# An order of single operations written out as a table, in place of a planner's, in a one-core attention and gated-MLP kernel

## The chip, the cores and the metric

One Trainium2 core. TensorE (PE) multiplies matrices, VectorE (DVE) and ScalarE (ACT) work on elements, GpSimd (POOL) does element work on SBUF alone, SyncE (SP) issues all the transfers. The metric is the device time of one execution in microseconds (us); lower is better.

## The reference

```python
# B = H = 4, S = 1088, D = 32, r = 8, d_model = 128, d_ff = 1024
a, b = S1 @ x, S2 @ x                       # 8 features each, per position
phi(x) = outer(a, b).reshape(64)
kv  = einsum('bhsf,bhsd->bhfd', phi(k), v);  z = phi(k).sum(s)
num = einsum('bhsf,bhfd->bhsd', phi(q), kv); den = phi(q) . z + 1e-6
x   = (num / den) -> (B, S, 128)
h   = relu(x @ w_in);  u, v = h[..., :512], h[..., 512:]
v_n = (v - mean(v)) / sqrt(var(v) + 1e-6)
v_s = einsum('ts,bsd->btd', w_spatial, v_n) + b_spatial
out = (u * v_s) @ w_out
```

## The kernel before

**Arithmetic.** Every product of the MLP is made in three matmuls: each factor is a rounded high part and the remainder as a low part (names in h and l: `wih`/`wil`, `xh`/`xl`, `vh`/`vl`, `wTh`/`wTl`), and high x high, high x low and low x high are summed in PSUM. `mm3` is that for products of x (L516 to L518); for the mixing of positions with `w_spatial` the three are L1092, L1094 and L1101. `w_in`, `w_out` and the S matrices arrive as 64-bit floats and are turned into 32-bit ones on the chip: for each half of `w_in` one ACT operation (the absolute value, L577) and six on VectorE (L580 to L590), then the split (L594 the high part, L526 the low).

**Stages.** For batch 0 (`attention0`): keys are projected (L674), copied by ACT (L679) and multiplied out to features on VectorE (L681, 128x768 a piece); a matrix product with v gives the 64 x 33 sums; queries the same way, turned by PE (L800), the quotient on VectorE (L818 to L833). Then the hidden v half for batch 0: `pv` products (L516 to L518 with `wi`), ReLU on ACT (L948), statistics on VectorE (L950), normalization and split into `vh` and `vl` (L1039 is vl's subtraction). With these, the mixing begins: `spatial` sums nine blocks of positions for each of 4 x 3 tiles (d, c) in a PSUM bank, `hidden` makes u (a bank `pu`, ACT's L1084 reads it), `gate` multiplies (L1128), `out_mm` multiplies with `w_out` (banks `po`). The attention of batch b+1 runs beside the mixing of batch b: `kv` (L724) sums keys with values on PE; a copy on ACT (L766), the four block products `kd` on VectorE (L907), a split into `kvh` (L594) and `kvl` (L526) follow, and then `nd` on PE (numerators and denominators, L516 with `area`) needs both. Query features are made on GpSimd: a product `fa` (L867) and the low part `fl` (L529). Batch 3 uses an algorithm with fewer products (`main_fast`).

**Order.** The code records operations, each with its engine, what it reads and writes. `schedule` then lists them in one order, and each engine runs its share of it in that order; PE fills some waits in the startup with small matmuls that nothing reads (L543), after N_WARM = 8 at the very start (L539). Before, `schedule` is a planner: it gives each operation a cost and a due time, `LEADS` moves due times by a few hundred numbers, and the operation that can start first goes next, the more urgent of two near each other. An operation marked `sh` reads two SBUF tiles on VectorE (or works in a mode of that sort); `pin` on a GpSimd operation adds a wait for the last `sh` operation ordered ahead of it, and is set for the query products of batches 2 and 3:

```python
s = max(s, shared_to + (66 if o.pin else -40))          # a GpSimd operation's planned start
...
o.behind = shared if o.pin else None                    # becomes a real wait
...
op("POOL", c_pool(n), ..., r=[fb], w=[fa], pin=b >= PIN_FROM)      # PIN_FROM = 2
```

SBUF and PSUM tiles live in groups of buffers (`po` 3, `sp` 2, `pu` 1, `sd` 2 in PSUM), used in turn.

Of the kernel before, what the change touches and what calls it, by code (L numbers as in the profile page):

```python
# [50 lines left out]
N_WARM = 8  # L51
# [23 lines left out]
SLACK = {'PE': 32, 'ACT': 56, 'DVE': 106, 'POOL': 890, 'SP': 84}  # L75

C_MM = {260: 120.5, 276: 127.0, 332: 146.8, 424: 186.8, "x1": 153.0, "rp": 150.5, 384: 174.7, 320: 146.0, 512: 231.5}
SETTLE = {332: (0, 5.1, 10.2, 14.5, 17.5, 20.1, 22.9, 24.8, 26.7, 28.3, 29.3, 30.3, 31.2, 31.7, 32.2), 424: (0, 6.4, 13.4, 18.1, 19.9, 21.9, 23.3, 24.3, 25.2, 25.6)}  # L80
STICK, PAUSE = 0.0, 30.0
HBM_LAG = (0, 500)
PIN_FROM, LATER = 2, 300.0

FILL_COLD, COLD_TO = 500, 7000
FILL, FILL_TO, FILL_SPARE = 430, 50.0, 150
FIRST_RATE, LOW_DELAY = 0.18, 4.4


class T:  # L90


    def __init__(self, k, tag, name, shape, dt):
        self.k, self.tag, self.name, self.shape, self.dt = k, tag, name, shape, dt
        self.users, self.left, self.free_at, self.slot, self._ap = [], 0, 0.0, None, None
        if tag is not None:
            k.fifo.setdefault(tag, []).append(self)

    @property
# [36 lines left out]
class Order:  # L136
# [13 lines left out]
    def op(self, eng, cost, fn, r=(), w=(), due=None, kb=0, alts=(), sh=False, kind=None, after=0.0, lead=0.0, f4=False, cls=None, lag=0.0, pin=False):  # L150
        o = Op()
        o.n, o.eng, o.fn, o.due, o.kb, o.f4 = len(self.ops), eng, fn, due, kb, f4
        o.lag, o.pin, o.behind = lag, pin, None
        o.cls, o.nmm = cls or ("f4" if f4 else "", 1)
        o.alts = ((eng, cost, fn), *alts)
        name = next(((x[0] if isinstance(x, tuple) else x).name for x in w), "out")
        self.named[name] = self.named.get(name, 0) + 1
        o.name = f"{name}:{self.named[name]}"
        if kind:
            o.alts = tuple(a for a in o.alts if a[0] in FORCE.get(kind, [eng]))  # L160
            o.eng, _, o.fn = o.alts[0]
            assert o.alts, kind
        o.stretch, o.sh, o.after, o.lead = self.stretch, sh, after * 1e3, lead + sum(LEADS.get(x, 0) for x in (*self.part, o.name))
        deps = {}
        r, w = ([(t, key) for t0, key in (x if isinstance(x, tuple) else (x, None) for x in xs) for t in (t0.tiles if isinstance(t0, Whole) else [t0])] for xs in (r, w))

        def split(x):
            return x if isinstance(x, tuple) else (x, None)

        def sets(a, c):  # L170
            return isinstance(a, frozenset) and isinstance(c, frozenset)

        def touching(table, t, key):
            for (t2, k2), v in table.get(t, {}).items():
                if key is None or k2 is None or (key & k2 if sets(key, k2) else k2 == key):
                    yield (t2, k2), v

        def within(k2, key):
            return key is None or (k2 <= key if sets(key, k2) else k2 == key)

        for x in r:
            t, key = split(x)
            for _, d in touching(self.last_w, t, key):
                deps[d] = True
        for x in w:
            t, key = split(x)
            for _, d in touching(self.last_w, t, key):
                deps[d] = True
            for _, ds in touching(self.readers, t, key):
                for d in ds:  # L190
                    deps[d] = True
        for x in r:
            t, key = split(x)
            self.readers.setdefault(t, {}).setdefault((t, key), []).append(o)
        for x in w:
            t, key = split(x)
            for k, _ in list(touching(self.last_w, t, key)):
                if within(k[1], key):
# [12 lines left out]
        for t in o.tiles:  # L211
            if t.tag is not None:
                o.first.append(t)
                t.users.append(o)
        self.ops.append(o)
        return o

    OV = {"ACT": 94, "DVE": 84, "POOL": 42, "PE": -165, "SP": 0}

    def schedule(self):  # L220
        ops = self.ops
        for o in reversed(ops):
            eng, cost, _ = o.alts[0]
            own = max(cost - self.OV[eng], 20) if eng != "PE" else cost + 165
            if eng == "SP":
                own = cost + 2000 + o.kb / 0.39 + o.lag
            own *= o.stretch
            dues = [s.due - own - self.LAT.get((eng, s.eng), 35) for s in o.succ]
            if o.due is not None:
                dues.append(o.due)  # L230
            o.due = round((min(dues) if dues else 1e9) - o.lead)
        free = {"PE": 1300.0, "ACT": 1080.0, "DVE": 830.0, "POOL": 700.0, "SP": 740.0}
        avail = {e: [] for e in free}
        taken = {tag: 0 for tag in self.fifo}
        slots = {tag: [(0.0, i) for i in range(self.bufs(tag))] for tag in self.fifo}
        for tag, ts in self.fifo.items():

            ts[:] = sorted((t for t in ts if t.users), key=lambda t: (t.users[0].n, t.users[0].first.index(t)))
            for n, t in enumerate(ts):
                t.n = n  # L240
                t.left = len(t.users)
        for o in ops:
            o.left, o.ready = len(o.deps), {}
            if not o.left:
                self.offer(o, avail)
        dma, slow, fetch = 0.0, False, list(FETCH)
        lanes = []
        pool_busy, shared_to, shared = (0.0, 0.0), 0.0, None
        f4, cls, run = True, "f4", 0
        order = []  # L250
        left = len(ops)
        while left:
            best = None
            for e, os in avail.items():
                can = []
                lo = 1e18
                for o in os:
                    s = max(free[e], self.ready_at(o, e))

                    if e == "POOL":  # L260
                        s = max(s, shared_to + (66 if o.pin else -40))
                    ok = True
                    need = {}
                    for t in o.first:
                        if t.slot is None:
                            need.setdefault(t.tag, []).append(t)
                    for tag, ts in need.items():
                        n = len(ts)
                        if [t.n for t in ts] != list(range(taken[tag], taken[tag] + n)) or n > len(slots[tag]):
                            ok = False  # L270
                            break
                        s = max(s, slots[tag][n - 1][0])
                    if ok:
                        can.append((s, o))
                        lo = min(lo, s)
                if can:
                    d, s, n, o = min((o.due + STICK * (e == "PE" and o.cls != cls), s, o.n, o) for s, o in can if s <= lo + SLACK[e])
                    if best is None or s < best[0]:
                        best = (s, e, o)
            if best is None:  # L280
                raise RuntimeError("no operation can start: " + str({e: [(x.n, [t.name for t in x.first]) for x in v][:4] for e, v in avail.items()}))
            s, e, o = best
            if len(o.alts) > 1:
                s, e = min((self.could_end(o, a, free), a[0]) for a in o.alts)
                s = max(free[e], self.ready_at(o, e), best[0] if e == best[1] else 0)
# [7 lines left out]
            for x in o.alts:  # L293
                avail[x[0]].remove(o)
# [89 lines left out]
def c_pool(n):  # L384
    return 90 + 2.4 * n
# [1236 lines left out]
```

## Time and profile before

| | before |
|---|---|
| median of 3 runs | 324.59 us (323.65 to 324.91) |
| the profiled execution | 324.06 us |
| its span in the trace | 322.3 us |
| PE busy | 314.4 us of it (98%) |
| DVE, ACT, POOL busy | 238.6, 175.3, 47.9 us |
| mean granted clock of PE | 0.998 |

The span is from the first to the last instruction that the profiler saw; the execution's own time is 1.76 us longer. Busy time counts work, not waiting, and matmuls overlap in the pipeline, so busy 98% doesn't mean that all of it is useful: the warm-up and fill matmuls count too.

### The profile page before, as it was taken

To read this page: it belongs to the slowest core of one execution; us is meant where nothing else is said; L and a number is where in the kernel's file an instruction comes from. 1 tells how busy PE (TensorE), PEld (TensorE's weight loads), DVE (VectorE), ACT (ScalarE), POOL (GpSimd) and SP (SyncE) were. 2 spreads that over 40 slices of the span, in tenths; PEclk is the share of its full clock that TensorE was granted. 3 is DMA by queue.
4 is the path that set the end of the run, shared out by engine and by line. 5 is a ranking of instruction groups with operands and counts; after the bars stand their busy time and mean duration, and the time that the engine had idled before them with its cause. 6 is when DMAs were issued, how large, how long until landed. Compare 5 with 4: busy or idle time off the path is not lost.

```text
span 322.3 us, 7124 instructions
## 1 busy us (share of the span) xinstructions
PE 314.4 (98%) x2723; PEld 300.7 (93%) x2723; DVE 238.6 (74%) x553; ACT 175.3 (54%) x422; POOL 47.9 (15%) x61
## 2 busy tenths in 40 slices
PE   8899999999999999999999999999999999999996
PEld 7787999999889899999989999999999999999995
DVE  4799999445698982569898299999998778551155
ACT  2299876535665563675346576664643565452241
POOL 2000001575311004450000652000000000000000
PEclk9999999999999999999999999999999999999999
DMA  6942168864011255200104453232223451000001
GB/s 203 294 126 90 54 168 240 262 190 151 0 49 46 87 153 165 84 2 24 46 16 127 129 166 93 71 81 61 77 83 88 132 158 29 2 0 2 0 21 52
DMA packets 26020, 30.78 MB, mean 96 GB/s; under 512 B 3330, under 2 KB 25730, under 8 KB 25986
## 3 DMA queue, kind: packets, MB, share of 16 engines
q1 hardware_dynamic: 25986, 30.33, 31.6%
q8 instruction: 21, 0.34, 0.5%
q14 instruction: 13, 0.11, 0.1%
HBM read 27.25 MB, written 3.06 MB: 94 GB/s over the span
## 4 chain that ended last, share of the span: by engine, by line
PE 90%; DVE 6%; ACT 2%; issue 1%; DVEq 0%; ACTq 0%
PE sp L1092 14%; PE sp L1101 12%; PE sp L1094 12%; PE sd L516 4%; PE sd L518 3%; PE sd L517 3%; PE pu L516 3%; PE sd L1364 3%; PE sd L1366 3%; PE sd L1365 3%; PE pu L517 2%; PE pu L518 2%; PE sp L1364 2%; PE sp L1366 2%; PE sp L1365 2%; PE sd L674 2%
## 5 line engine op out<-in xcount | busy, mean ns | idle before, releaser
L1092 PE MATMUL sp<-wT,vh 128*128 128x332 f32 (+1 forms) x306 | 99.5, 325 | 0.8 <-DVE u L1128 0.8
L1094 PE MATMUL sp<-wT,vl 128*128 128x332 f32 (+1 forms) x272 | 87.7, 322 | 0.0
L1101 PE MATMUL sp<-wT,vh 128*128 128x332 f32 (+1 forms) x272 | 85.7, 322 | 0.0
L1092 PEld LDWEIGHTS sp<-wT,vh 128*128 128x128 f32 x306 | 57.5, 188 | 3.1 <-DVE u L1128 1.5
L1094 PEld LDWEIGHTS sp<-wT,vl 128*128 128x128 f32 x272 | 51.1, 188 | 0.4
L1101 PEld LDWEIGHTS sp<-wT,vh 128*128 128x128 f32 x272 | 51.1, 188 | 0.1
L948 ACT ACTIVATE vt<-sd 128x512 f32<-128x512 f32 x36 | 21.4, 599 | 12.9 <-PE sd L518 12.2
L1128 DVE TENSOR_TENSOR u<-sp,u 128x332 f32<-128x332 f32 (+1 forms) x32 | 16.6, 520 | 14.6 <-PE sp L1103 12.1
L526 DVE TENSOR_TENSOR g<-u,g 128x332 fp32r<-128x332 f32 (+1 forms) x32 | 17.8, 557 | 12.8 <-PE po L517 9.8
L950 DVE BATCH_NORM_STATS2 small<-vt 128x6 f32<-128x512 f32 x36 | 24.3, 685 | 3.9 <-ACT vt L948 3.9
L928 DVE RECIPROCAL area<-area 128x384 f32<-128x384 f32 (+1 forms) x9 | 21.7, 2416 | 7.1 <-ACT area L926 7.1
L867 POOL TENSOR_TENSOR area<-area 128x384 f32<-128x384 f32 (+1 forms) x18 | 17.7, 992 | 50.8 <-DMA area<-abd 24.0
L594 ACT CAST g<-u 128x332 fp32r<-128x332 f32 (+1 forms) x32 | 15.4, 488 | 13.4 <-DVE u L1128 9.1
L1084 ACT ACTIVATE u<-pu 128x332 f32<-128x332 f32 (+1 forms) x32 | 14.9, 467 | 13.0 <-PE pu L518 9.8
L529 POOL TENSOR_TENSOR area<-area,area 128x384 fp32r<-128x384 f32 (+1 forms) x18 | 17.6, 985 | 17.2 <-ACT area L594 17.2
L516 PE MATMUL pu<-x,wih 128*128 128x332 f32 (+3 forms) x52 | 17.1, 329 | 0.8 <-ACT area L1084 0.6
L649 POOL TENSOR_TENSOR wT<-area,wT 128x332 fp32r<-128x332 f32 (+1 forms) x9 | 8.2, 929 | 56.7 <-DMA area<-in_vA 51.9
L517 PE MATMUL pu<-x,wih 128*128 128x332 f32 (+3 forms) x52 | 16.4, 314 | 0.0
L518 PE MATMUL pu<-x,wil 128*128 128x332 f32 (+3 forms) x52 | 16.3, 314 | 0.0
L681 DVE TENSOR_TENSOR area<-ka,sd 128x768 f32<-128x768 f32 x15 | 13.7, 944 | 2.8 <-ACT ka L679 2.5
L970 DVE TENSOR_SCALAR vt<-vt,small 128x512 f32<-128x512 f32 x32 | 15.6, 539 | 0.0
L516 PE MATMUL sd<-wi,x 128*128 128x512 f32 x36 | 14.7, 409 | 0.0
(237 smaller groups left out, 764.3 us busy)
## 6 DMA issues: line engine op xcount, KB each, us to landing
w<-in_wT SPq DMA_DIRECT2D x48, 138.0 KB
area<-in_wT SPq DMA_DIRECT2D x18, 166.0 KB
area<-in_vA SPq DMA_DIRECT2D x12, 198.0 KB
area<-in_kT SPq DMA_DIRECT2D x12, 192.0 KB
area<-abd SPq DMA_DIRECT2D x12, 192.0 KB
area<-abd SPq DMA_DIRECT2D x24, 96.0 KB
area<-in_wT SPq DMA_DIRECT2D x9, 212.0 KB
area<-in_qT SPq DMA_DIRECT2D x7, 192.0 KB
```

Source lines behind the costliest of these rows:

```text
L516: nc.tensor.matmul(o, ah, bh, start=start, stop=False)
L517: nc.tensor.matmul(o, ah, bl, start=False, stop=False)
L518: nc.tensor.matmul(o, al, bh, start=False, stop=stop)
L526: return lambda: nc.vector.tensor_tensor(out=o(), in0=a(), in1=bb(), op=ALU.subtract)
L529: return lambda: nc.gpsimd.tensor_tensor(out=o(), in0=a(), in1=bb(), op=ALU.subtract)
L867: op("POOL", c_pool(n), lambda fa=fa, fb=fb: nc.gpsimd.tensor_tensor(out=fa[:, :n], in0=fa[:, :n], in1=fb[:, :n], op=ALU.mult), r=[fb], w= ...
L928: op("DVE", 135 + 6.3 * n, lambda x32=x32, n=n: nc.vector.reciprocal(out=x32[:, :n], in_=x32[:, :n]), w=[x32])
L948: op("ACT", c_act(512, True) + 16, lambda pv=pv, t=t: nc.scalar.activation(vt[:, t], pv.ap, AF.Relu), r=[pv], w=[(vt, toks(t))])
L950: op("DVE", 690, lambda stats=stats, t=t: nc.vector.bn_stats(out=stats.ap, in_=vt[:, t]), r=[(vt, toks(t))], w=[stats])
L1092: nc.tensor.matmul(sp[:, :cw], vh[:, kt], wTh[:, kt, cs], start=(kt == 0), stop=False)
L1094: nc.tensor.matmul(sp[:, :cw], vl[:, kt], wTh[:, kt, cs], start=False, stop=False)
L1101: nc.tensor.matmul(sp[:, :cw], vh[:, kt], wTl[:, kt, cs], start=False, stop=False)
```

## The change

The planner goes, with `LEADS`; a table `ORDER` of 1,912 operation numbers takes its place. A number followed by an apostrophe runs on its other engine; `po0` and `po1` in it are fill matmuls. `schedule` walks it and hands out buffers as they come free. `pin` is now the default, so each GpSimd operation waits for the last `sh` operation of VectorE ordered ahead of it; `kd` becomes `sh`; `v90` to `v93` get tiles of their own. N_WARM is 7, and there are 5 fills in place of 7. Four operations change engine: `vl00:3` from VectorE to GpSimd, `vt02:4` and `vt02:5` (two of batch 0's normalizations) from VectorE to ACT, `vt02:6` from ACT to VectorE. The changed costs (`load_wi`, `phi`) act on nothing, since the table sets the order.

```diff
-N_WARM = 8
+N_WARM = 7
-LEADS = {'S1': 3520, 'S1.00': -6080, ...}
+LEADS = {}
+ORDER = """
+0 1 2 3 4 5 10 13 14 11 6 12 15 56 37 7 8 16 17 18 19 20 21 22 59 60 61 43 44 45 39 po0 47 48 49 27 28 29 30 31 32 23 po1 po1 po1 po1 68 41 51 69 52 58 70 65 38 40 53 42 57 202 46
...
+"""
-    def op(self, eng, cost, fn, ..., lag=0.0, pin=False):
+    def op(self, eng, cost, fn, ..., lag=0.0, pin=True):
     def schedule(self):
-        ...                                    # the planner
+        left, free = {}, {tag: list(range(self.bufs(tag))) for tag in self.fifo}
...
+        order, done, shared = [], set(), None
+        for x in ORDER.split():
+            if x[0].isalpha():
+                home = x[:2], int(x[2:])
+                order.append(Fill(lambda home=home: self.fill(*home)))
+                continue
+            o = self.ops[int(x.rstrip("'"))]
+            o.eng, _, o.fn = o.alts[x[-1] == "'"]
             for t in o.first:
                 if t.slot is None:
+                    t.slot = free[t.tag].pop(0)
+            if o.eng == "POOL":
+                o.behind = shared
+            if o.eng == "DVE" and o.sh:
+                shared = o
...
-            op("POOL", c_pool(n), ..., r=[fb], w=[fa], pin=b >= PIN_FROM)
+            op("POOL", c_pool(n), ..., r=[fb], w=[fa])
-                op("DVE", 215, part, r=[kv, mask], w=[(kd, (pr, den))])
+                op("DVE", 215, part, r=[kv, mask], w=[(kd, (pr, den))], sh=True)
```

Lines of the changed kernel are those of before less 56 (L681 becomes L625). Three places show what moved. On SP, the start of the program, before (`in_sks` the S matrices, `in_kT` and `in_qT` keys and queries of batch 0, `in_idn` an identity, `in_vA` values, `in_w_in` a half of `w_in`):

```order
1 L523 DMA area_79<-in_sks 128x128
2 L523 DMA area_78<-in_kT 128x384 x3
3 L523 DMA area_79<-in_idn 128x128
4 L523 DMA area_79<-in_qT 128x384
5 L523 DMA area_78<-in_vA 128x396
6 L523 DMA vt<-in_w_in 128x1024
7 L523 DMA area_78<-in_vA 128x396 x2
```

and of the change:

```order
1 L467 DMA area_79<-in_sks 128x128
2 L467 DMA area_79<-in_qT 128x384
3 L467 DMA area_78<-in_kT 128x384 x2
4 L467 DMA vt<-in_w_in 128x1024
5 L467 DMA area_79<-in_idn 128x128
6 L467 DMA area_78<-in_kT 128x384
7 L467 DMA area_79<-in_qT 128x384
8 L467 DMA area_78<-in_vA 128x396 x3
```

The first half of `w_in` is now fifth of the transfers, with four ahead of it; it was eighth. On VectorE, the place behind the S matrices' conversion, before (`sd` the projected keys or queries, `vt` the half of `w_in`):

```order
11 L681 TENSOR_TENSOR area_78<-ka_63,sd_126 128x768
12 L681 TENSOR_TENSOR area_78<-ka_70,sd_94 128x768
13 L681 TENSOR_TENSOR area_78<-ka_63,sd_126 128x768
14 L681 TENSOR_TENSOR area_78<-ka_70,sd_94 128x768
15 L580 TENSOR_SCALAR vt<-vt 128x512
16 L582 TENSOR_SCALAR vt<-vt 128x512
17 L583 SCALAR_TENSOR_TENSOR vt<-vt 128x512
```

and of the change:

```order
11 L625 TENSOR_TENSOR area0_78<-ka0_63,sd1_117 128x768
12 L625 TENSOR_TENSOR area0_78<-ka1_70,sd0_93 128x768
13 L625 TENSOR_TENSOR area0_78<-ka0_63,sd1_117 128x768
14 L524 TENSOR_SCALAR vt_82<-vt_82 128x512
15 L526 TENSOR_SCALAR vt_82<-vt_82 128x512
16 L527 SCALAR_TENSOR_TENSOR vt_82<-vt_82 128x512
17 L532 TENSOR_SCALAR vt_82<-vt_82 128x512
18 L625 TENSOR_TENSOR area0_78<-ka1_70,sd0_93 128x768
```

The conversion of `w_in` begins after three feature products, not four; the fourth now stands inside it. On PE, what follows the last `kv` products of batch 1, before (`wT` mixing, `g` and `x` with `wo` the output product, `pu` hidden u):

```order
220 L724 MATMUL sd0_94<-area0_78 32x33 x72
221 L516 MATMUL po2_258<-g_782,woh_69 128x332
222 L517 MATMUL po2_258<-g_782,woh_69 128x332
223 L518 MATMUL po2_258<-g_782,wol_73 128x332
224 L1092 MATMUL sp1_282<-wT_74,vh_67 128x332
225 L1094 MATMUL sp1_282<-wT_74,vl_71 128x332
226 L1101 MATMUL sp1_282<-wT_74,vh_67 128x332
```

and of the change:

```order
256 L668 MATMUL sd1_117<-area0_78 32x33 x72
257 L460 MATMUL po2_261<-x_77,woh_69 128x424
...
262 L462 MATMUL po2_261<-x_77,wol_73 128x424
263 L1036 MATMUL sp1_275<-wT_74,vh_67 128x332
264 L1038 MATMUL sp1_275<-wT_74,vl_71 128x332
265 L1045 MATMUL sp1_275<-wT_74,vh_67 128x332
266 L460 MATMUL pu0_185<-x_77,wih0_68 128x332
267 L461 MATMUL pu0_185<-x_77,wih0_68 128x332
268 L462 MATMUL pu0_185<-x_77,wil0_72 128x332
269 L460 MATMUL sd0_93<-area2_80 128x384
```

The first `nd` (the last row) used to stand 29 matmuls behind `kv`; now 12 stand between them.

## Rows read from the trace of the kernel before

**Rows 1.** The page, busy times, and the shares of the chain that ended last.

```profile
PE 314.4 (98%) x2723; PEld 300.7 (93%) x2723; DVE 238.6 (74%) x553; ACT 175.3 (54%) x422; POOL 47.9 (15%) x61
...
PE 90%; DVE 6%; ACT 2%; issue 1%; DVEq 0%; ACTq 0%
```

**Rows 2.** Windows: stretch, its us, busy us of each engine (instructions), PEclk, DMA, GB/s.

```profile
5.05:12.24 7.19, 6.53 (x117) 5.73 (x117) 3.73 (x5) 2.02 (x6) 0.00 (x0) 1.00 0.96 291
12.24:32.56 20.32, 18.60 (x160) 15.38 (x157) 20.11 (x56) 15.93 (x39) 0.00 (x0) 1.00 0.45 143
...
80.00:100.00 20.00, 19.19 (x116) 17.77 (x115) 16.72 (x34) 13.68 (x30) 4.53 (x5) 1.00 0.06 20
...
220.00:240.00 20.00, 19.73 (x124) 19.32 (x123) 19.24 (x49) 9.56 (x24) 0.00 (x0) 1.00 0.25 70
```

**Rows 3.** PE's waits: for what, total us, times, longest.

```profile
PE po L800 <- DVE area L681: 1.1, 3, 0.5
PE sp L1092 <- DVE u L1128: 0.8, 2, 0.6
```

**Rows 4.** Timeline of PE: start, us, tile and form; the first row's narrow window.

```profile
4.06 1.06 PE L539 MATMUL sd<-first 128*128 128x128 f32 x4
5.05 0.48 PE L674 MATMUL sd<-sk,area 128*64 128x64 f32 x4
...
32.99 0.35 PE L1092 MATMUL po<-wT,vh 128*128 128x424 f32 x1
...
41.96 0.36 PE L516 MATMUL pu<-x,wih 128*128 128x424 f32 x1
...
42.54 0.35 PE L1092 MATMUL sp<-wT,vh 128*128 128x424 f32 x1
```

**Rows 5.** Timeline of DVE and ACT in the startup.

```profile
9.55 0.95 DVE L681 TENSOR_TENSOR area<-ka,sd 128x768 f32<-128x768 f32 x1 [0.29 <-PE pu L712]
12.24 0.43 DVE L580 TENSOR_SCALAR vt<-vt 128x512 f32<-128x512 f32 x1 [1.74 <-ACT vt L577]
...
0.73 1.28 ACT L548 ACT_TABLE_LOAD   x1 [0.73 <-PEq L1610]
2.02 0.20 ACT L548 ACTIVATE small<-first 1x1 f32<-1x1 f32 x1
...
11.14 0.48 ACT L804 COPY area<-po 128x384 f32<-128x384 f32 x1 [2.14 <-PE po L800]
11.52 0.69 ACT L577 ACTIVATE vt<-vt 128x512 f32<-128x512 f32 x1
```

**Rows 6.** SP's waits in the first 40 us, and its timeline.

```profile
SPq L523 <- DMA vt<-in_w_in: 2.1, 1, 2.1
...
10.50 0.33 SPq L523 DMA_DIRECT2D u<-in_qT  x1
```

**Rows 7.** PE's and DVE's timeline behind kv of batch 1; L907 by line.

```profile
67.90 0.31 PE L1092 MATMUL sp<-wT,vh 128*128 128x332 f32 x1
...
71.74 0.35 PE L516 MATMUL sd<-area 128*128 128x384 f32 x1
...
67.98 1.54 DVE L907 TENSOR_TENSOR area<-ka,small 128x64 f32<-128x64 f32 x4 [2.57 <-ACT ka L766]
70.05 0.43 DVE L526 TENSOR_TENSOR area<-area,area 128x256 fp32r<-128x256 f32 x1 [0.53 <-ACT area L594]
...
L907 DVE TENSOR_TENSOR area<-ka,small x12: 214/219/1133, 68.0 to 170.4; 128x64 f32<-128x64 f32 x12
```

**Rows 8.** PE's longest wait in the mixing: timelines of DVE, POOL and PE; L929 by line.

```profile
79.95 1.37 DVE L929 TENSOR_TENSOR area<-area 128x384 f32<-128x384 f32 x1
...
79.63 1.28 POOL L529 TENSOR_TENSOR area<-area,area 128x384 fp32r<-128x384 f32 x1
...
81.80 0.42 PE L1092 MATMUL sp<-wT,vh 128*128 128x332 f32 x1 [0.56 <-DVE u L1128]
...
L929 DVE TENSOR_TENSOR area<-area x9: 492/558/1372, 80.0 to 207.5; 128x384 f32<-128x384 f32 x6, 128x320 f32<-128x320 f32 x3
```

More of the change, by code (lines that the diff above doesn't have):

```diff
@@ L87 @@
 FIRST_RATE, LOW_DELAY = 0.18, 4.4
+ORDER = """
+0 1 2 3 4 5 10 13 14 11 6 12 15 56 37 7 8 16 17 18 19 20 21 22 59 60 61 43 44 45 39 po0 47 48 49 27 28 29 30 31 32 23 po1 po1 po1 po1 68 41 51 69 52 58 70 65 38 40 53 42 57 202 46
+50 66 9 24 54 71 62 203 211 178 193 187 175 102 63 33 101 207 190 181 67 55 103 34 72 35 64 81 82 73 74 75 92 79 76 90 212 36 213 204 214 80 77 78 215 91 83 194 188 179 116 117 112
+120 84 216 85 217 86 218 118 113 93 87 219 88 94 114 121 119 182 89 115 95 122 104 191 176 96 123 141 124 220 125 97 133 126 105 142 143 134 352 127 353 189 135 128 144 137 129 138
+139 136 366 367 98 99 205 221 106 100 206 210 208 109 131' 381 184 382 154 140 130 145 285 132 177 146 147 286 162 396 148 155 291 163 297 180 107 199 149 292 158 159 290 287 289
+293 150 108 196 164 288 294 295 298' 296 302 299 301 300 160 165 156 152 157 161 151' 303 153' 185 304 166 167 168 169 170 171 305 307 306 308 309 315 172' 200 321 222 310 312 311
+313 197 195 316 314 320 186 322 318 183 173' 327 192 174 326 317 333 323 319 325 328 249 336 255 256 324 329 338 331 332 341 209 372 339 330 373 342 374 375 387 223 201 340 388 389
[42 rows of a table added]
+"""
 class T:
@@ L148, in tile, with op @@
         return T(self, tag, name, shape, dt)
-    def op(self, eng, cost, fn, r=(), w=(), due=None, kb=0, alts=(), sh=False, kind=None, after=0.0, lead=0.0, f4=False, cls=None, lag=0.0, pin=False):
+    def op(self, eng, cost, fn, r=(), w=(), due=None, kb=0, alts=(), sh=False, kind=None, after=0.0, lead=0.0, f4=False, cls=None, lag=0.0, pin=True):
         o = Op()
@@ L220, in schedule @@
     def schedule(self):
[L221 to L235, printed above, removed]
-        for tag, ts in self.fifo.items():
[L238 to L285, printed above, removed]
-            _, cost, fn = next(a for a in o.alts if a[0] == e)
-            if e == "PE" and s < FILL_TO * 1e3:
-                n = int((s - free[e] - FILL_SPARE) // (FILL if s > COLD_TO else FILL_COLD))
-                home = next(((tag, i) for tag in ("po", "sp", "pu") for t, i in slots[tag] if t <= free[e]), None)
-                if n > 0 and home:
-                    order += [Fill(lambda home=home: self.fill(*home))] * n
-            for x in o.alts:
-                avail[x[0]].remove(o)
-            o.eng, o.fn, o.start = e, fn, s
@@ new lines, in schedule @@
+        left, free = {}, {tag: list(range(self.bufs(tag))) for tag in self.fifo}
+        for tag, ts in self.fifo.items():
+            ts[:] = [t for t in ts if t.users]
+            for t in ts:
+                left[t] = len(t.users)
+        order, done, shared = [], set(), None
+        for x in ORDER.split():
+            if x[0].isalpha():
+                home = x[:2], int(x[2:])
+                assert home[1] in free[home[0]]
+                order.append(Fill(lambda home=home: self.fill(*home)))
+                continue
+            o = self.ops[int(x.rstrip("'"))]
+            assert o not in done and done.issuperset(o.deps)
+            o.eng, _, o.fn = o.alts[x[-1] == "'"]
@@ L296, in schedule @@
             for t in o.first:
                 if t.slot is None:
-                    t.slot = slots[t.tag].pop(0)[1]
-                    taken[t.tag] += 1
-            if e == "PE":
-                s += TURN * (o.f4 != f4)
-                f4 = o.f4
-                if o.cls != cls or s > free[e] + PAUSE:
-                    run = 0
-                cls, run = o.cls, run + o.nmm
-                settle = SETTLE.get(cls, (0,))
-                cost += settle[min(run, len(settle) - 1)] - settle[min(run - o.nmm, len(settle) - 1)]
-                o.end = s + cost + 165
-                free[e] = s + cost
-            elif e == "SP":
-                dma = max(dma, s + cost + 1950)
-                took = o.kb / ((0.30 if dma > 20000 else 0.38) if o.kb > 0 else -0.12)
-                while fetch and fetch[0] < dma + took:
-                    f = fetch.pop(0)
-                    if dma < f + 1450:
-                        dma, took = (f + 1450, took) if f < dma else (dma, took + 1450)
-                dma += took
-                if dma > 5000 and not slow:
-                    slow, dma = True, dma + 1400
-                o.end = dma + o.lag
-                lanes.append(o.end)
-                free[e] = max(s + cost, lanes[-8] if len(lanes) >= 8 else 0)
-            else:
-                o.end = s + cost
-                if e == "DVE" and o.sh and pool_busy[0] <= s < pool_busy[1] - 20:
-                    o.end = max(o.end, pool_busy[1] + cost - 60)
-                if e == "POOL":
-                    pool_busy = (s, o.end)
-                    o.behind = shared if o.pin else None
-                if e == "DVE" and o.sh:
-                    shared_to, shared = o.end, o
-                free[e] = o.end - self.OV[e]
@@ L336, in schedule @@
-            left -= 1
+                    t.slot = free[t.tag].pop(0)
[3 more added lines that the diff above has]
+                shared = o
+            done.add(o)
             order.append(o)
@@ L339, in schedule @@
                 if t.tag is not None:
-                    t.left -= 1
-                    t.free_at = max(t.free_at, o.end + 60)
-                    if not t.left:
-                        insort(slots[t.tag], (t.free_at, t.slot))
-            for x in o.succ:
-                x.left -= 1
-                if not x.left:
-                    self.offer(x, avail)
-        return order
-    @staticmethod
-    def offer(o, avail):
-        for a in o.alts:
-            avail[a[0]].append(o)
-    def ready_at(self, o, e):
-        if e not in o.ready:
-            o.ready[e] = max([d.end + (-165 if d.eng == e == "PE" else self.LAT.get((d.eng, e), 35)) for d in o.deps], default=0.0)
-            o.ready[e] = max(o.ready[e], o.after)
-        return o.ready[e]
-    def could_end(self, o, a, free):
-        return max(free[a[0]], self.ready_at(o, a[0])) + a[1]
+                    left[t] -= 1
+                    if not left[t]:
+                        free[t.tag].append(t.slot)
+        assert len(done) == len(self.ops)
+        return order
     def size(self, tag):
@@ L468, in tile_kernel @@
         end += n
+    const.tile([P, 8], F32, name="pad4")
+    fixed |= {f"v9{d}": const.tile([P, P], F32R, name=f"v9{d}") for d in range(ND)}
     def gates():
@@ L622, in load_wi @@
         sl = slice(j * 512, j * 512 + 512)
-        load(raw, lambda: raw[:, :1024].bitcast(U32), w_in[:, sl].bitcast(U32), 1000 if j else 560)
+        load(raw, lambda: raw[:, :1024].bitcast(U32), w_in[:, sl].bitcast(U32), 560)
         from_f64(x, raw, 512)
@@ L634, in blank @@
             z = z9[:, :NS * 12].rearrange("p (k c) -> p k c", k=NS)
-            nc.gpsimd.tensor_tensor(out=t[:, :, GAP], in0=z, in1=z, op=ALU.subtract)
+            return nc.gpsimd.tensor_tensor(out=t[:, :, GAP], in0=z, in1=z, op=ALU.subtract)
         op("POOL", 360, blank, r=[z9], w=[tl(None, f"gap_{t.name}", [1, 1]), (t, "gap")], due=8000)
@@ L690, in phi @@
         ab = bank("sd", f"{what}ab{b}{g}")
-        op("PE", 353, f4=True, fn=lambda: project(ab, xt), r=[xt, (sk, "x")], w=[ab])
+        op("PE", 353 + {"k00": 270, "k01": 150}.get(f"{what}{b}{g}", 0), f4=True, fn=lambda: project(ab, xt), r=[xt, (sk, "x")], w=[ab])
         return features(b, g, ab, what)
@@ L866, in expanded @@
                 op("SP", 610, lambda fb=fb, a=a, r=r: nc.sync.dma_start(out=fb[64 * a:64 * a + 64, :n], in_=abd[r:r + 8].unsqueeze(0).broadcast_to([R, R, n])), r=[abd], w=[(fb, a)], kb=n // 4, lag=HBM_LAG[1] + LATER * (b >= PIN_FROM))
-            op("POOL", c_pool(n), lambda fa=fa, fb=fb: nc.gpsimd.tensor_tensor(out=fa[:, :n], in0=fa[:, :n], in1=fb[:, :n], op=ALU.mult), r=[fb], w=[fa], pin=b >= PIN_FROM)
+            op("POOL", c_pool(n), lambda fa=fa, fb=fb: nc.gpsimd.tensor_tensor(out=fa[:, :n], in0=fa[:, :n], in1=fb[:, :n], op=ALU.mult), r=[fb], w=[fa])
             query_fs[b, g, pr] = fa
@@ L906, in part @@
                     src = (v[:, :, D:] if den else v[:, :, :D]).broadcast_to([P, 2, D])
-                    nc.vector.tensor_tensor(out=kd[:, 1 + pr if den else 3 * pr], in0=src, in1=mask[:, 2:4].unsqueeze(2).broadcast_to([P, 2, D]), op=ALU.mult)
-                op("DVE", 215, part, r=[kv, mask], w=[(kd, (pr, den))])
+                    return nc.vector.tensor_tensor(out=kd[:, 1 + pr if den else 3 * pr], in0=src, in1=mask[:, 2:4].unsqueeze(2).broadcast_to([P, 2, D]), op=ALU.mult)
+                op("DVE", 215, part, r=[kv, mask], w=[(kd, (pr, den))], sh=True)
         kvh, kvl = tl("kvh", f"kvh{b}", [P, 2, P], F32R), tl("kvl", f"kvl{b}", [P, 2, P], F32R)
@@ L969, in dve @@
             def dve(t=t):
-                v.tensor_scalar(out=vt[:, t], in0=vt[:, t], scalar1=mv[:, t, 0:1], scalar2=rs[:, t:t + 1], op0=ALU.subtract, op1=ALU.mult)
+                return v.tensor_scalar(out=vt[:, t], in0=vt[:, t], scalar1=mv[:, t, 0:1], scalar2=rs[:, t:t + 1], op0=ALU.subtract, op1=ALU.mult)
             def act(t=t):
```

1 line of the change is left out of this document (removed), and 42 rows, old and new, of the table ORDER.

## The prediction

> **What bounds the kernel now.** I read the page first, then windows by stage, PE's waits, and the timelines where PE waits. The page has PE busy for 314.4 of 322.3 us, and the chain that ended last is 90% PE and 6% VectorE [rows 1]: the change makes PE do the same products, so it can only win what PE spends on waiting, on fill and on warm-up. In most of the mixing there is nothing to win. The windows with idle time are the startup, 80 to 100 us (19.19 busy of 20) and 220 to 240 (19.73 of 20) [rows 2].
>
> In the startup PE looks busy, but VectorE sets the pace: from the first conversion step of `w_in` at 12.24 to the end of the first `vl` subtraction at 32.56 VectorE is busy 20.11 of 20.32 us [rows 2]. The mixing starts right behind it, at 32.99 [rows 4]. And the conversion starts at 12.24 because VectorE waits 1.74 us for ACT's L577, which starts at 11.52 behind the copy L804 [rows 5]. The half of `w_in` had landed by about 10.5: SP's next issue stood 2.1 us for that transfer and went at 10.50 [rows 6]. So the order of first loads and first conversions is on the path that sets the end.
>
> **The change, part by part.** The sum is made against the profiled 324.06 us (span 322.3, 1.76 outside); the median of the runs, 324.59, stands 0.53 above, and I carry that over.
>
> *Startup.* The conversion's transfer is now fifth, not eighth, with 64 + 3 x 192 KB ahead instead of about 1,090 KB. At the 291 GB/s of 5.05 to 12.24 [rows 2] about 450 KB less is 1.6 us, a landing near 8.9; the bound on the one side is 10.5 (no earlier, if later transfers share the way as before), on the other 6.5 (nothing shares it). ACT's absolute value takes 0.69 [rows 5] and no longer stands behind L804, which made it start 1.0 us after the landing; so VectorE could begin at about 9.6. It can't begin before its third feature product is done, near 8.9: the fourth ended at 10.50 before (9.55 + 0.95) [rows 5], and one product of 0.95 and a gap go. I take 9.5, 2.7 earlier than 12.24, and keep 8.9 and 11.2 (10.5 + 0.69) as ends. From there to the first `vl` VectorE now has 55 operations, not 54: the fourth feature product (0.95) and a small subtraction (0.17, from like ones) come in, one of 0.12 goes. So the work is 21.1 us, it ends at 30.7, and the mixing starts 0.43 later, as now, near 31.1: 1.8 sooner. Ahead of that PE has also done one bank `pu` that stood at 41.96 before, worth 0.58 (41.96 to 42.54) [rows 4]. Startup: **2.3 us** (ends 0.6 and 3.0). What PE does itself doesn't limit this: 18.60 of the 20.32 us are busy, fills and the waits on VectorE among it, and one warm-up fewer lets PE begin sooner (four matmuls take 1.06 there, and a warm-up is two of them, so at most 0.5) [rows 4], where they wait for transfers anyway; that I cost at nothing.
>
> *Second table load.* In the changed ACT order the square root's dummy, with its table load, is no longer first but stands behind five copies and the absolute value, and a first load for the copies stays. So one load of 1.28 and the dummy of 0.20 [rows 5] come to lie near 11 us, ahead of the second turned-query copy. That copy feeds a quotient that VectorE reaches only behind the first conversion, so some 0.8 us of cover remain: cost nothing, and without the cover at most 0.7. The Trainium skill, page "ScalarE: Activation LUTs", section "What ACT_TABLE_LOAD costs", counts about 1.38 us of drain on top of a load; the trace shows the next ACTIVATE at 2.02, directly behind the load's end at 2.01, so the row decides, and by the page the sum would be 0.7 worse.
>
> *Old waits in the mixing.* PE's long wait for `gate` (0.56 at 81.80) is due to VectorE's L929: it took 1.37 beside GpSimd's L529 of 79.63 to 80.91, against a median of 0.558 [rows 8]. The table sets GpSimd work elsewhere. With it go the rest of 80 to 100 (0.81 idle in all) and 0.27 of 220 to 240 [rows 2]: **1.1 us** (ends 0 and 1.1).
>
> *New waits.* Behind `kv` of batch 1 the chain was: copy, four `kd`, cast, `kvl`, done at 70.48, which is 2.6 after the 67.90 at which PE had gone on to the mixing; the first `nd` came at 71.74, 3.84 after 67.90, so it cost nothing [rows 7]. Now 12 matmuls stand in between, two output products of a 424-wide tile (0.58 each by row 41.96), a block of 0.45 and a `pu` of 0.45, 2.07 us in all. The `kd` operations took 1.54 for four, with one of 1133 ns among medians of 219 [rows 7]; as `sh` operations that GpSimd waits behind, they may take 0.9, and the chain from the end of `kv` 2.4. So PE waits 0.3 there (ends 0 and 1.0). For waits of this kind at other places that I can't place I take as much again: **-0.6** (ends 0 and 3: ten like it).
>
> *Turns of form.* PE changes between its two number forms 17 times, not 21, and between shapes of product 215, not 241; a first matmul behind a turn takes 0.42 where its neighbours take 0.31 (the one at 81.80 against the one at 67.90) [rows 7, 8]. That is 30 turns fewer at 0 to 0.1 each, most of them hidden in the pipeline; I take an estimate of 0.007 for one: **0.2** (ends 0 and 3).
>
> Extra waits of GpSimd for VectorE are costed at nothing: GpSimd is busy for 47.9 us [rows 1], and of PE's waits none is on it [rows 3]; what it costs without that cover is the third rival.
>
> The sum: 324.06 - 2.3 - 1.1 + 0.6 - 0.2 = 321.06; with 0.53 for the median 321.6, and I say 321.5.
>
> **The rivals.** *The change doesn't do what it says: VectorE still runs beside GpSimd.* The added wait holds a GpSimd operation behind an earlier VectorE operation; nothing holds a later VectorE operation back while GpSimd still runs. Then L929 and `kd` stay as long as now, 0.56 + 0.3 us are not won and `nd` waits up to 0.7 more: 322.9. The Trainium skill, page "SBUF — State Buffer", section "Who interferes with whom", says just this: issue order decides who is blocked, and whoever issues first holds the shared pair for the whole instruction. The trace agrees with its mechanism (1.37 against 0.558, 1133 against 219 ns) [rows 7, 8]. But outside the three windows named PE has no idle time to speak of, so only few such places are on its path.
>
> *The startup's gain is given back.* PE with 2.3 us more to do by 80 us meets VectorE, ACT and the `nd` chain that much earlier; a pipeline that is held by transfers of `w_spatial` or by VectorE's 96% in 220 to 240 (19.24 of 20) [rows 2] takes it as new waits. For it: VectorE is nearly full in both those windows. Against: its load before 240 falls, since it has two operations fewer, and PE was never short of a transfer in the mixing. 324.59 - 2.3 + 2.3 - 0.3 = 324.3.
>
> *Slower: GpSimd's waits reach PE.* Each of the 36 large GpSimd operations (`fa` and `fl`) now waits for the last shared VectorE operation ahead of it, also in batch 1. If VectorE stands behind PE at that place, GpSimd's 1 us comes behind it, and `nd` waits for `fl`. Six query tiles by two such waits of 0.6 would be 7.2: 324.59 - 2.3 + 7.2 - 1.1 = 328.4. It decides from a total of about 5.0 us of new waits on. For it: these operations were free to start early before. Against: no wait of PE is on GpSimd now [rows 3], and GpSimd is 85% idle.
>
> **How the numbers follow.** My forecast has 0.53, VectorE beside GpSimd 0.14, gain given back 0.21, slower 0.12. What a measurement can tell from no change is 0.5%, or 1.6 us: 322.97 and 326.21 are the bounds. The first two are faster: 0.67. The third is the same: 0.21. The fourth is slower: 0.12. The startup's ends give 321.6 + 1.7 = 323.3 and 321.6 - 0.7 = 320.9; with the ends of new waits (+2.4, -0.6) and old ones (+1.1) root-sum-squared upward that is 3.1, downward 0.9, so 320.7 to 324.7. Where it comes out above 322.9 it is the second or third case; the forecast's own range is 320.4 to 322.9. The range for 8 in 10 reaches up to the third case, 324.4, and down to 319.4, which a third of the bound on turns of form, and startup and new waits at their better ends, would give.
>
> **What would show it.** The mixing's first matmul (L1036) near 31.1, with VectorE busy without a gap from about 9.5; the window 80 to 100 without its 0.8 us idle; behind `kv` of batch 1 an idle of 0.3 before the first `nd`, put down to VectorE or ACT. The prediction is wrong if `w_in`'s half still lands at 10.5, if VectorE has gaps of over 1 us before the first `vl`, if PE's list of waits has over 2 us from 33 to 316, or if GpSimd is named in it.

## The result and the profile after

The changed kernel takes 319.6 us (319.48 to 319.69, 4 runs), the kernel before 324.51 in the same comparison: ratio 0.985, 95% interval 0.983 to 0.987, 4.9 us faster. A second comparison gave 320.0 (ratio 0.987, 0.986 to 0.989). 321.5 was forecast, with 319.4 to 324.4 as the range, so 319.6 lies only just inside its lower end.

The page of the changed kernel, busy times and chain, against [rows 1]:

```profile
PE 312.5 (98%) x2717; PEld 299.7 (94%) x2717; DVE 238.3 (75%) x551; ACT 173.0 (54%) x424; POOL 47.4 (15%) x62
...
PE 95%; DMA 3%; DVE 1%; SPq 1%; issue 0%; DVEq 0%
```

PE's busy share is 98% as before; the span fell from 322.3 to 317.8. VectorE's share of the chain fell from 6% to 1%. The windows of [rows 2], and one from the first conversion step to the first mixing product of the changed kernel (columns as there):

```profile
80.00:100.00 20.00, 20.00 (x128) 19.32 (x127) 17.22 (x39) 13.00 (x31) 4.90 (x7) 1.00 0.19 60
220.00:240.00 20.00, 20.00 (x120) 19.94 (x119) 17.45 (x45) 7.78 (x20) 0.00 (x0) 1.00 0.23 60
9.23:31.62 22.39, 21.94 (x221) 18.01 (x220) 21.58 (x57) 18.40 (x41) 0.00 (x0) 1.00 0.54 171
```

Both windows are now without idle time on PE. All of PE's waits in the changed kernel:

```profile
PE sd L483 <- DVE first L479: 1.3, 1, 1.3
PE sp L758 <- DVE area L721: 0.4, 1, 0.4
PE po L744 <- DMA area<-in_idn: 0.3, 1, 0.3
PE sd L618 <- DVE area L625: 0.2, 1, 0.2
```

All four lie in the first 14 us. The waits on `gate` and on ACT are gone, and nothing in the list replaced them. The startup, timelines of VectorE, ACT and PE:

```profile
9.23 0.43 DVE L524 TENSOR_SCALAR vt<-vt 128x512 f32<-128x512 f32 x1 [0.56 <-ACT vt L521]
...
8.52 0.67 ACT L521 ACTIVATE vt<-vt 128x512 f32<-128x512 f32 x1 [0.84 <-DMA vt<-in_w_in]
...
11.18 1.28 ACT L492 ACT_TABLE_LOAD   x1
12.47 0.20 ACT L492 ACTIVATE small<-first 1x1 f32<-1x1 f32 x1
...
25.25 0.36 PE L460 MATMUL pu<-x,wih 128*128 128x424 f32 x1
...
31.62 0.35 PE L1036 MATMUL po<-wT,vh 128*128 128x424 f32 x1
```

The conversion starts at 9.23 (12.24 before), the mixing at 31.62 (32.99), and PE has done four `pu` banks by then, where it had done three.

To see where the time came from, I counted the useful matmuls (all but warm-ups and fills; 296.6 us in either kernel, each at its median distance to the next one in the kernel before) that had started by a time. The lead of the changed kernel, in us:

```
t           33    80    100   220   240   last matmul
lead        1.9   2.4   3.9   4.1   4.6   4.6
```

So 1.9 us come from the startup, 0.5 from 33 to 80, 1.5 from 80 to 100, 0.7 from 100 to 240. In the profile of the second comparison the lead is 2.3 at 33 and 4.4 at the last matmul, so 2.1 come from behind the startup there, and 0.2 of them from 33 to 80. From profile to profile of the same kernel a stretch differs by up to 0.4.

### The profile page after: what moved, and what is told of

The parts are those of the page before. It is cut to its first block, busy times and chain, and to the rows that moved or that the text cites. A ratio compares the mean times of both kernels' runs of the same rounds, so it can differ in the third digit from the quotient of the medians.

```text
span 317.8 us, 7095 instructions
## 1 busy us (share of the span) xinstructions
PE 312.5 (98%) x2717; PEld 299.7 (94%) x2717; DVE 238.3 (75%) x551; ACT 173.0 (54%) x424; POOL 47.4 (15%) x62
## 4 chain that ended last, share of the span: by engine, by line
PE 95%; DMA 3%; DVE 1%; SPq 1%; issue 0%; DVEq 0%
PE sp L1036 16%; PE sp L1038 14%; PE sp L1045 14%; PE sd L460 4%; PE sd L461 4%; PE sd L462 4%; PE pu L460 3%; PE sd L1308 3%; PE sd L1310 3%; PE sd L1309 3%; PE pu L461 3%; PE pu L462 2%; PE po L460 2%; PE sp L1309 2%; PE sp L1310 2%; PE sp L1308 2%
## 5 line engine op out<-in xcount | busy, mean ns | idle before, releaser
L625 DVE TENSOR_TENSOR area<-ka,sd 128x768 f32<-128x768 f32 x15 | 13.7, 947 | 4.9 <-ACT ka L623 4.8
L590 ACT CAST wT<-area 128x332 fp32r<-128x332 f32 (+1 forms) x27 | 12.5, 497 | 8.0 <-DMA area<-in_wT 7.9
L952 ACT CAST vh<-vt 128x384 fp32r<-128x384 f32 x24 | 12.1, 515 | 6.8 <-DVE vt L914 6.8
```

## The experiments

**Start and rest, and the waits of GpSimd.** First a control: the changed code with the old order as its table. Then the two orders cut at the first mixing product and crossed; and the changed order with GpSimd's waits as before. (In all runs that begin in the changed order, the repeat of the change apart, four of the five fills also write `po0` in place of `po1`; the run with `kd` unshared, at 319.93, shows no cost of that.)

```diff
 # t0_old_order, h1_new_start, h2_new_body: the operations of ORDER in
-changed order
+old order | changed order to the first mixing product, the rest in the old | the reverse
 # t0_old_order, h1_new_start, e_old_pins:
-lag=0.0, pin=True):
+lag=0.0, pin=False):
-                o.behind = shared
+                o.behind = shared if o.pin else None
-r=[fb], w=[fa])
+r=[fb], w=[fa], pin=b >= PIN_FROM)
-r=[kv, mask], w=[(kd, (pr, den))], sh=True)
+r=[kv, mask], w=[(kd, (pr, den))])
```

> The changed code with a table that holds the order and the engines of the kernel before (its fills too, seven warm-ups, waits of GpSimd as before). If the order alone carries the change: 324.3 (324.0 to 324.7), PE's waits of 0.56 at 80 to 82 us and 0.27 at 227 us are back. Rival (tiles of their own for v90 to v93, buffers handed out as they come free, or the missing warm-up carry a part): under 323.5.

> The table is the changed one up to the first mixing product; all operations that are left follow in the order of the kernel before. If start and rest are worth something each by themselves: 324.5 - 1.9 = 322.6 (322.2 to 323.0), with mixing from 31.6 us on and PE's waits near 80 and 227 us still there. Rival (an earlier start is given back in the body): 324 or more, with new waits of PE behind 33 us.

> The reverse: the order of the kernel before up to the first mixing product, the rest in the changed order, GpSimd waiting as in the change. If the parts add: 319.6 + 1.9 = 321.5 (321.1 to 322.0), mixing from 33.0 us on, PE without a wait from there to 300 us. Rival (the body's gain hangs on the earlier start): 323 or more.

> The changed order, but GpSimd's added waits behind VectorE as in the kernel before (only the query products of batches 2 and 3), and kd not counted as shared. If the waits carry nothing: 319.6 (319.3 to 319.9). Rival (they keep GpSimd off VectorE's operations on PE's path): 320.2 or more, with VectorE's lengthened operations above the 4.0 us in 8 operations of the change.

Measured, each with the kernel before at 324.31 beside it: control 324.77 (ratio 1.001, 1.000 to 1.002); new start 323.36 (0.997, 0.9955 to 0.9987); new body 324.04 (0.999, 0.998 to 1.000); old waits 320.96 (0.990, 0.989 to 0.992).

The control has the old order and the old waits, so it shows that these two carry the change between them, and no other part of the code: it is no faster than before. Of the two waits that I named, the one on `gate` is back (0.6); the one near 227 us is not in its list. It is not a clean copy, though. Its mixing starts later: PE waits 1.6 us for ACT at its third `pu` (0.6 in the kernel before), and the cause is open.

The parts don't add by the medians. The new start is 0.95 us faster than before (0.4 to 1.5), the new body 0.3, together 1.2 of the 4.4 to 4.9. The profiles show a part of the reason: a cut puts operations in the wrong place at the seam. With the new start, PE's lead is 1.1 us at 33 and gone at 50 (-0.4), by these waits from 33 to 300 us:

```profile
PE sp L1031 <- DVE u L1067: 0.5, 1, 0.5
PE po L1031 <- ACT area L792: 0.4, 1, 0.4
PE pu L455 <- ACT u L1023: 0.3, 1, 0.3
PE sp L1033 <- DVE vl L978: 0.3, 1, 0.3
```

The second and last are the seam's, and the old wait on `gate` is there. With the new body PE is 1.5 us behind the kernel before at 40: it waits the control's 1.6 us, and 0.9 more at a `pu` that the changed order has ahead of the cut and that now comes behind it. From 40 us to the last matmul it wins 2.6, where the changed kernel wins 2.7 (1.9 to 4.6) and 2.3 in its second profile. So in this execution the body's gain doesn't hang on the start. But it was the fastest of the ten runs (323.26), as the control's profiled one was the slowest of its ten (325.66); by medians the new body is 0.7 faster than the control, which starts in the same order, and 324.04 is where the rival had it (323 or more). How much of the body's gain other executions keep behind the old start is open. Nor does the new start show that the start's gain survives by itself: half of it is left in 323.36.

The old waits cost 0.9 to 1.6 us (0.990 against 0.987 and 0.985; the first of these intervals overlaps that of the old waits, the second doesn't): my theory that they carry nothing fell. The sign that I had named for the rival came too: VectorE operations over 0.1 us above the median of their form are 11 here, with 7.4 us above it in all, against 8 with 4.0. What the old waits do at `kd` of batch 1, timeline of VectorE with the old waits, and in the changed kernel; then the wait of PE with the old ones:

```profile
69.66 2.01 DVE L846 TENSOR_TENSOR area<-ka,small 128x64 f32<-128x64 f32 x4 [2.05 <-ACT ka L705]
```

```profile
69.47 0.84 DVE L851 TENSOR_TENSOR area<-ka,small 128x64 f32<-128x64 f32 x4 [2.24 <-ACT ka L710]
```

```profile
71.31 0.31 PE L457 MATMUL pu<-x,wil 128*128 128x332 f32 x1
72.16 0.44 PE L455 MATMUL sd<-area 128*128 128x384 f32 x1 [0.54 <-ACT area L533]
```

Four `kd` operations take 2.01 instead of 0.84, the cast for `nd` comes later, and PE stands. There is a second place. With the old waits GpSimd makes the `vl` that the change gave it earlier, beside VectorE's small operations, and one of these takes 1.26 us where its like take 0.15:

```profile
31.84 1.26 DVE L900 SCALAR_TENSOR_TENSOR small<-small 128x3 f32<-128x3 f32 x1
```

```profile
31.72 1.36 POOL L978 TENSOR_TENSOR vl<-vt,vh 128x512 fp32r<-128x512 f32 x1 [29.40 <-ACT vh L975]
```

By the distance between starts of matmuls the first place costs PE 0.8 us; near 36 us three starts come 0.5 later in all than their like, which I take for the effect of the second.

**The other corner, the first load, and kd alone.** The old order with the new waits; the changed kernel with the first half of `w_in` late, behind four more transfers; the changed kernel with `kd` not shared; the changed kernel again.

```diff
 # e_late_wi, in ORDER (27 is the load of the half of w_in; 23 the identity, 41 keys, 58 queries, 38 values)
-47 48 49 27 28 29 30 31 32 23 ...
+47 48 49 23 41 58 38 27 28 29 30 31 32 ...
 # e_kd_unshared
-r=[kv, mask], w=[(kd, (pr, den))], sh=True)
+r=[kv, mask], w=[(kd, (pr, den))])
```

> The changed kernel once more, as the reference for the others of this group: 319.6 (319.3 to 320.0).

> The order of the kernel before, as in the first group's control (324.8), but every GpSimd operation waits behind the last shared VectorE operation ordered ahead of it, kd among them. Theory (the waits keep GpSimd off the VectorE operations that PE needs, in either order): 323.4 (323.0 to 323.9), kd of batch 1 in about 0.9 us, the L929 kind back to 0.56 and PE's 0.56 wait near 82 us gone. Rival (the waits help only with the order that was made for them): 324.6 or more.

> The changed kernel with the first half of w_in as the eighth transfer, as before, behind the identity, the third keys and queries and the first values; nothing else moves. If its landing sets the start: VectorE's conversion begins some 1.6 us later and the time is 321.0 (320.6 to 321.5). Rival (PE is full by then and the delay is absorbed): 319.6 to 320.0.

(The edit makes it the ninth transfer, not the eighth: both the second load of queries and the third of keys now stand ahead of it. That is 646 KB more ahead than in the change, 2.2 us at the 291 GB/s of [rows 2], where I had 1.6.)

> The changed kernel, kd no longer counted as shared, all other added waits kept. If kd's lengthening by GpSimd is what the old waits cost: kd of batch 1 takes about 2.0 us in place of 0.84, PE waits 0.5 for the first nd and the time is 320.3 (320.1 to 320.7). Rival (the other waits carry it): 319.6 to 319.9.

Measured beside 324.43 of before: 320.0 for the change; old order with new waits 324.1 (0.9994, 0.9985 to 1.0003); late `w_in` 324.42 (0.999, 0.997 to 1.002; 321.21 to 326.05 in 10 runs); `kd` unshared 319.93 (0.987, 0.985 to 0.988).

`kd`'s mark costs and brings nothing: without it the four take 0.63 in the profile, and 0.63 in the second profile of the changed kernel too. GpSimd's next operation starts behind `kvl` in both (`kvl` is `sh` by itself), at 71.10 and 71.09. In the old order the waits bring 0.7 us in medians (324.77 to 324.1), on intervals that overlap at their ends, so neither the 323.4 of the theory nor the rival's 324.6 came. The place is that of [rows 8], which the control repeats with the old waits: VectorE's L868 there, and GpSimd.

```profile
81.82 1.37 DVE L868 TENSOR_TENSOR area<-area 128x384 f32<-128x384 f32 x1
...
81.50 1.28 POOL L468 TENSOR_TENSOR area<-area,area 128x384 fp32r<-128x384 f32 x1
```

and with the new waits:

```profile
80.94 0.55 DVE L868 TENSOR_TENSOR area<-area 128x384 f32<-128x384 f32 x1
...
81.57 0.88 POOL L806 TENSOR_TENSOR area<-area 128x320 f32<-128x320 f32 x1 [2.92 <-DVE area L868]
```

GpSimd now waits until L868 is done, L868 takes 0.55, and `gate`'s wait is gone from PE's list.

The late `w_in` cost 4.4 us, three times what I expected. VectorE's conversion starts 1.9 us later than in the changed kernel's second run, whose row is the second:

```profile
10.64 0.43 DVE L519 TENSOR_SCALAR vt<-vt 128x512 f32<-128x512 f32 x1 [2.44 <-ACT vt L516]
```

```profile
8.73 0.43 DVE L524 TENSOR_SCALAR vt<-vt 128x512 f32<-128x512 f32 x1
```

The fourth feature product stands behind four steps of it in VectorE's order, so the third `kv` product has to wait. PE's timeline, and windows:

```profile
13.63 0.92 PE L651 MATMUL pu<-area 128*64 128x66 f32 x24 [2.23 <-DVE area L620]
```

```profile
10.00:12.00 2.00, 1.40 (x42) 1.16 (x38) 1.29 (x3) 1.98 (x5) 0.00 (x0) 1.00 0.99 315
12.00:14.00 2.00, 0.37 (x12) 0.37 (x14) 1.97 (x4) 1.23 (x4) 0.00 (x0) 1.00 0.90 303
14.00:16.00 2.00, 1.84 (x35) 1.65 (x31) 2.00 (x5) 0.35 (x2) 0.00 (x0) 0.63 0.84 280
16.00:18.00 2.00, 2.00 (x12) 2.00 (x12) 0.71 (x1) 0.50 (x1) 0.00 (x0) 0.50 0.76 227
18.00:20.00 2.00, 2.00 (x11) 2.00 (x11) 1.65 (x5) 1.06 (x2) 0.00 (x0) 0.50 0.32 103
20.00:24.00 4.00, 4.00 (x25) 3.52 (x23) 3.23 (x10) 3.30 (x7) 0.00 (x0) 0.83 0.01 4
```

PE stands for 2.23 us, and after that it was granted 0.50, the lower of its two levels (1.2 GHz), for nearly 7 us (from within the 0.63 to within the 0.83). So there were two candidates for the 4.4: the delay and the clock.

**Delay or clock.** The same late transfer, with fill matmuls where PE stood.

```diff
 # in ORDER of e_late_wi, ahead of 54 (the third kv product of batch 0)
-50 66 9 24 54 71 ...
+50 66 9 24 po2 po2 po2 po2 po2 po2 po2 po2 po2 54 71 ...      # 9; 14 in e_late_wi_fills
```

> The late transfer of the first half of w_in once more (324.42 without fills), with 14 small matmuls that nothing reads put where PE stood idle for 2.2 us, ahead of the third kv product of batch 0. If the idle stretch lowers PE's clock and that carries most of the loss: granted clock 1.00 throughout and 321.3 (320.8 to 321.8), that is only the later landing's 1.2 to 1.6. Rival (the loss is VectorE's delay itself): 324 or more, with the clock at 1.00.

> As the late transfer with fills, but 9 fills (0.24 us each by the 3.39 us of 14, so 2.2 us, the idle time) in place of 14, which were 1.1 us too many and went with a stall of 2.3 us on instruction issue near 74 us. If the idle stretch's clock carries most of the loss: clock 1.00, no stall on issue, 321.3 (320.8 to 321.8). Rival (the stall on issue comes with any added instructions): the same stall again and 323.3 or more, clock 1.00. Third (VectorE's delay carries the loss by itself): 323.5 or more without that stall.

Fourteen fills: 324.45 (1.000, 0.998 to 1.001), with the clock at 0.999. That speaks against the clock, but the run was muddled twice: the fills took 3.39 us where 2.2 were wanted, and near 74 us PE stood for nothing that the profile names (in the one execution that was profiled):

```profile
PE po L455 <- issue: 2.3, 1, 2.3
```

Nine fills: 322.18 (0.992, 0.990 to 0.994), clock 0.998 to 1.000 in all six runs, no such stall. So with the clock held the late landing costs 1.5 to 2.2 us (0.992 against 0.987 and 0.985), and the clock about 2.2 more. In the nine fills' profile, the slowest of the six, the conversion starts at 11.47, later than the 10.64 above, so the landing varies between runs of the same order of loads. The late kernel's own runs agree: seven at a mean clock of 0.989 took 323.98 to 325.38 and one at 0.984 took 326.05, while two at 0.999 and 1.000 took 322.84 and 321.21; whether PE stood as long in these two isn't known.

**The second table load, and the identity.**

```diff
 # e_one_table, in ORDER (9 is the square root's dummy)
-0 1 2 3 4 5 ... 50 66 9 24 ...
+0 1 2 9 3 4 5 ... 50 66 24 ...
 # e_idn_early (23 is the identity's load)
-47 48 49 27 28 29 30 31 32 23 ...
+47 48 49 23 27 28 29 30 31 32 ...
```

> The changed kernel with the square root's dummy first on ACT, as before, so that one table load is left. If the second load (1.28 and the dummy's 0.20 near 11.2 us) is hidden: 319.8 (319.5 to 320.1). Rival (it delays the turned queries and with them PE): 319.4 or less.

> The changed kernel with the identity's transfer (64 KB) ahead of the half of w_in, not behind it. If PE's first turn of the queries waits for it: PE's wait of 0.3 on in_idn goes, w_in lands 0.2 later, 319.6 (319.3 to 319.9). Rival (w_in's landing counts for more): 320.0 to 320.4.

Measured: 320.33 (0.9875, 0.985 to 0.990) and 320.34 (0.987, 0.985 to 0.989), against 0.987 of the change's second comparison. Neither can be told from it. The table load is hidden, as costed: without it ACT's copy L743 starts at 10.91 (12.58 in the changed kernel), but PE's next wait, for L721, is not on it. In the changed kernel the ACTIVATE behind the load starts at 12.47, where the load of 11.18 ends, so no more than the costed 1.28 and 0.20 lies there. The 319.8 expected for one load was missed by 0.5 on the slow side. With the identity ahead, PE's wait of 0.3 for it goes, but PE then stands 0.7 us for the third load of keys; 320.34 is in the range of the rival there, though the noise covers the difference. No version tried was faster than the change beyond the noise.

## Why the prediction was right, and where it was short

**The startup, 2.3 us.** Measured 1.9 in one profile and 2.3 in the other (lead at 33 us). The steps held: `w_in` landed by 8.52 and 8.01 (8.9 forecast), the conversion began at 9.23 and 8.73 (9.5), and VectorE was busy for 21.58 of 22.39 us from there to the mixing. The mixing began at 31.62 and 31.06 (31.1), with one `pu` bank more behind it, as counted (0.58): for the first, 1.37 + 0.58 is 1.95. In the first profile VectorE began 0.3 sooner than forecast and the mixing 0.5 later, so the stretch that I had summed was 0.8 us too short. What I had not priced is the other side: with the transfer ninth this order loses all (324.42), half of it through the clock. I said that what PE does doesn't limit the startup. In the new order PE is busy for 21.94 of the 22.39 us (18.60 of 20.32 before) and its `kv` products hang on VectorE's conversion steps, so a late transfer reaches PE at once.

**The old waits, 1.1 us: mis-sized.** Three waits went, as forecast, but they were worth 1.9. The idle time that the profile shows for a wait is not what it costs. Around the wait of [rows 8], PE's timeline of before:

```profile
80.78 0.31 PE L1094 MATMUL sp<-wT,vl 128*128 128x332 f32 x1
80.92 0.31 PE L1101 MATMUL sp<-wT,vh 128*128 128x332 f32 x1
81.80 0.42 PE L1092 MATMUL sp<-wT,vh 128*128 128x332 f32 x1 [0.56 <-DVE u L1128]
82.05 0.31 PE L1094 MATMUL sp<-wT,vl 128*128 128x332 f32 x1
```

Matmuls start 0.15 apart in a run. Here 0.88 and 0.25 lie between starts, 0.73 and 0.10 more than that: 0.83 for a wait shown as 0.56. The same sum for the other two gives 0.51 and 0.55, against the usual 0.15 and, for the wider tile, 0.19:

```profile
89.72 0.32 PE L1101 MATMUL sp<-wT,vh 128*128 128x332 f32 x1
90.28 0.42 PE L516 MATMUL pu<-x,wih 128*128 128x332 f32 x1 [0.24 <-ACT u L1084]
90.53 0.32 PE L517 MATMUL pu<-x,wih 128*128 128x332 f32 x1
```

```profile
227.08 0.36 PE L518 MATMUL po<-g,wol 128*128 128x424 f32 x1
227.71 0.46 PE L1092 MATMUL sp<-wT,vh 128*128 128x424 f32 x1 [0.27 <-DVE u L1128]
228.00 0.35 PE L1094 MATMUL sp<-wT,vl 128*128 128x424 f32 x1
```

A matmul's duration in the trace (0.31) is twice the distance to the next start, so matmuls overlap, and idle time is counted only from the end of one. The first matmul behind a pause takes longer (0.42), and the next start comes later (0.25).

**New waits, -0.6: didn't come.** PE has no wait after 14 us. Behind `kv` of batch 1 I had the chain end with `kvl`. In the changed kernel `nd` starts at 71.08, while `kvl` is still being made:

```profile
71.08 0.34 PE L460 MATMUL sd<-area 128*128 128x384 f32 x1
...
70.78 0.42 DVE L470 TENSOR_TENSOR area<-area,area 128x256 fp32r<-128x256 f32 x1 [0.47 <-ACT area L538]
```

Its first product needs only the cast (`kvh`, done at 70.75), 0.4 earlier than the point I waited for; and `kd` took 0.84. The cover of 2.07 (2.15 in the trace, from 68.93 to 71.08) was enough, just: with the old waits the same place shows PE idle for 0.54.

**Turns of form, 0.2: not shown.** No run measures a turn by itself. The row that I read its price from, 0.42 at 81.80, isn't one: the matmul ahead of it (80.92, above) has the same form, and the 0.42 belongs to the pause. The 0.5 of 33 to 80 us (0.2 in the second profile) are the only part in which I can't name a wait that went; turns may be in it, and so may noise.

**GpSimd behind VectorE, nothing: wrong.** I costed the waits at nothing and had the order do the work. They are worth 0.9 to 1.6 us in the new order and some 0.7 in the old. The rival that VectorE would still run beside GpSimd is half true: VectorE operations over 0.1 us above the median of their form are 8 in number with 4.0 us above it in all, about as before (8 and 3.7; 6 and 3.4 in the second profile). But in this order the old waits make it 11 and 7.4, and the ones that are left moved. By line, `kd` and the quotient in the changed kernel:

```profile
L851 DVE TENSOR_TENSOR area<-ka,small x12: 210/217/432, 69.5 to 170.6; 128x64 f32<-128x64 f32 x12
```

```profile
L873 DVE TENSOR_TENSOR area<-area x9: 491/550/834, 75.9 to 206.2; 128x384 f32<-128x384 f32 x6, 128x320 f32<-128x320 f32 x3
```

The maxima were 1133 and 1372 [rows 7, 8]. The Trainium skill, page "SBUF — State Buffer", section "Who interferes with whom", says that issue order decides who is blocked; the two runs of the old order show it at one place (1.37 with GpSimd first, 0.55 with GpSimd held behind).

**Sum.** 2.3 + 1.1 + 0.2 - 0.6 was 3.0; the first trace has 1.9 + 2.7 = 4.6 (4.5 in span), the second 2.3 + 2.1 = 4.4 (4.3 in span). The direction and the startup were right, the body was short by 1.4 to 2.0: 0.8 on the size of waits and 0.6 on waits that didn't come; the 0.6 left over in the first trace is open and isn't in the second. That 319.6 lies in the range is partly luck. Its lower end allowed 0.8 more for turns of form, which no run shows; the old waits, which I had bounded at 1.1, won those 0.8 instead.

## What to carry to other kernels

Price a wait of a busy TensorE by the distance between the starts of the matmuls around it, not by the idle time shown: here it was 0.3 us more each time. Where GpSimd and VectorE share work near TensorE's path, hold GpSimd behind the VectorE operation that TensorE needs, and check by name which operations got longer, not only how many. A first load that is late can cost twice if TensorE falls idle on it, when the granted clock falls as well, as in eight of ten runs here; fill the gap, or order VectorE so that TensorE's work doesn't hang behind the late one.

## What I had not expected of the hardware

A pause of 2.2 us on PE near 12 us brought the granted clock down to 0.50 for nearly 7 us; pauses of 0.9 and 1.6 us in other runs (new start, control) did not, with mean clocks of 0.999 and 1.000. With fill matmuls in the long pause the mean clock was 0.998 to 1.000 in all sixteen runs. In the profile with fourteen added fills near 12 us there is a 2.3 us stall on issue at 74 us, with nine there is none; why is open.
